# A scan and mixture-of-adapters kernel: new step priorities and latencies in its list scheduler, a row-tiled fp32 warm-up, and the constants' cast on GpSimd

## The chip, the cores and the metric

The kernel runs on one core of a Trainium2 chip. The metric is device time in microseconds (us) of one execution, and a kernel's time is the median of its runs. The profile is a trace of one execution. Its span is about 2 us shorter than the timed run of the same kernel (211.1 against 213.3 before), so times are compared with times and spans with spans.

Engines: PE is TensorE (PEld its weight loads), DVE is VectorE, ACT is ScalarE, POOL is GpSimd, SP is SyncE, which issues all large loads and stores.

## The reference

Cut to what matters:

```python
def _attn_ref(a, b):                    # a, b: [8, 6400, 128] fp32
    h = np.zeros((B, D))
    for t in range(S):
        h = a[:, t] * h + b[:, t]
        out[:, t] = h
def _moe_ref(x, w_gate, A, B):          # x: [51200, 128]; 8 experts of rank 16
    logits = x @ w_gate
    topk = ...                          # the 2 largest of 8
    w = softmax over the two
    for e in range(E):
        delta[mask] += w[mask, k, None] * ((x[mask] @ A[e]) @ B[e])
    return x + delta                    # x is the scan's output
```

## The kernel before

The 51,200 rows are cut into 100 tiles of 512. A tile `w` goes through these steps, each of four PE instructions or of one on another engine:

| step | engine | work |
|---|---|---|
| A, B | PE | fp32 transposes of `a` and `b` into PSUM |
| aev | ACT | copies the transposed `a` to SBUF |
| scan | DVE | the recurrence, gives `x` in fp16 |
| L | PE | logits, then small gating steps on DVE, POOL and ACT for up to four tiles together |
| Z | PE | `x` times all 8 `A` |
| mul | DVE, 13 of 100 on POOL | gates times Z |
| T, tev | PE, ACT | transposes the product, copies it |
| R, D | PE | `x` itself, then the product times `B`, both into the output's bank |
| oev | ACT (last ten: ACT or DVE) | copies the output tile; SP stores two tiles at a time |

The order of instructions on each engine isn't written by hand. A list scheduler simulates the kernel with a duration per step and a latency per engine, and takes the step that can start first, or among equals the one with the smallest key.

```python
        for op in ops.values():
            op.key = 300.0 * op.key - rank[op.name]
        # ... cut ...
        free = {e: 0.0 for e in self.sems}
        # ... cut: the pick ...
                    if best is None or (t + late, x[1].key) < best[:2]:
                        best = (t + late, x[1].key, e, x, t)
        # ... cut ...
            if op.dma:
                link = max(link, t + busy + 1500.0) + op.dma[2] / dma_rate
                end[op.name] = link + op.lat[e]
            else:
                end[op.name] = t + busy + op.lat[e]
```

```python
    KZ, KT, KR, KD = 8, 8.2, 8.6, 8.0
    PM = 6
    # ... cut ...
    stores = cut((), 2, (1, 1))          # stores of two tiles, the last two of one
    # ... cut ...
            lat = {"pe": 190.0, "dve": 120.0, "act": 150.0, "pool": 100.0, "sp": 100.0}
    # ... cut ...
        def heat(h):
            for _ in range(5):
                last = h.matmul(pB[1][:, :], warm_t[:, 0:128], warm_t[:, :])
            return last

        add("heat", "pe", -9, 2200.0, heat, ["wt"])
        add("idh", "dve", -8, 230.0, lambda h: h.tensor_copy(ident_h[:, :], ident_f[:, :]), ["id"])
        add("cst", "dve", -8, 300.0, lambda h: h.tensor_copy(cst_h[:, :], cst_f[:, :]), ["cst_in"])
    # ... cut ...
        def on_pool(w):
            return w % PM == 3 and 8 < w < NU - 16
    # ... cut: if on_pool(w), ACT copies pZ to SBUF (zev) and POOL multiplies ...
            add(f"Z{w}", "pe", w + KZ, 230.0, emit, [f"scan{w}", f"mul{w - NZ}", f"zev{w - NZ}", "cst"])
            add(f"R{w}", "pe", w + KR, 226.0, emit_x, [f"scan{w}", f"oev{w - NO}", "idh"])
            add(f"D{w}", "pe", w + KD, 226.0, emit_d, [f"R{w}", f"tev{w}", "cst"])
```

Of the kernel before, what the change touches and what calls it, by code (L numbers as in the profile page):

```python
# [7 lines left out]
F32 = mybir.dt.float32  # L8
# [22 lines left out]
class _Plan:  # L31
# [24 lines left out]
    def schedule(self, dma_rate):  # L56
# [16 lines left out]
        free = {e: 0.0 for e in self.sems}  # L73
# [7 lines left out]
        while todo:  # L81
# [20 lines left out]
            if op.dma:  # L102
                link = max(link, t + busy + 1500.0) + op.dma[2] / dma_rate
                end[op.name] = link + op.lat[e]
            else:
                end[op.name] = t + busy + op.lat[e]
# [36 lines left out]
def bass_associative_scan_2x2__then__mixture_of_adapters_kernel(  # L143
# [24 lines left out]
    KZ, KT, KR, KD = 8, 8.2, 8.6, 8.0  # L168
    PM = 6
# [31 lines left out]
    with ExitStack() as stack:  # L201
# [6 lines left out]
        warm_t = sb(nc.sbuf_tensor("warm_t", [128, UT], F16))  # L208
        warm = sb(nc.sbuf_tensor("warm", [128, 1], F32))
# [40 lines left out]
        def add(name, eng, key, busy, emit, deps=(), dma=None, bank=None):  # L250
            lat = {"pe": 190.0, "dve": 120.0, "act": 150.0, "pool": 100.0, "sp": 100.0}
            plan.add(name, eng, key, busy, lat, emit, deps, dma, bank)

        def add_dma(name, eng, key, emit, slot, nbytes, deps=()):
            if slot not in dma_sem:
                dma_sem[slot] = [sb(nc.semaphore("q_" + "_".join(map(str, slot)))), 0]
            dma_sem[slot][1] += 16
            sem, value = dma_sem[slot]
            add(name, eng, key, 650.0, lambda h: emit(h).then_inc(sem, 16), deps, (sem, value, nbytes))


        add("id0", "pool", -9, 200.0, lambda h: h.memset(ident_f[:, :], 0.0))
# [3 lines left out]
            -9,  # L266
# [21 lines left out]
        add("cst_in", "act", -9, 1800.0, lambda h: cst_load(h).then_inc(s_cst, 16), (), (s_cst, 48, 200000))  # L288
        add("w0", "dve", -9, 60.0, lambda h: h.memset(warm[:, :], 0.0))
        add("table", "act", -8, 1500.0, lambda h: h.activation(warm[:, :], warm[:, :], ACTF.Sigmoid), ["w0"])  # L290
        add("wt", "dve", -9, 60.0, lambda h: h.memset(warm_t[:, :], 0.0))

        def heat(h):
            for _ in range(5):
                last = h.matmul(pB[1][:, :], warm_t[:, 0:128], warm_t[:, :])
            return last

        add("heat", "pe", -9, 2200.0, heat, ["wt"])
        add("idh", "dve", -8, 230.0, lambda h: h.tensor_copy(ident_h[:, :], ident_f[:, :]), ["id"])
        add("cst", "dve", -8, 300.0, lambda h: h.tensor_copy(cst_h[:, :], cst_f[:, :]), ["cst_in"])  # L300
# [19 lines left out]
        def transposes(kind, w):  # L320
# [12 lines left out]
            add(f"{kind}{w}", "pe", w - (0.3 if kind == "A" else 0), 440.0, emit, [f"ld{kind.lower()}{load_of[w]}", free, "id"])  # L333

        def a_evac(w):
# [3 lines left out]
                w,  # L339
# [5 lines left out]
        def scan(w):  # L345
# [4 lines left out]
            def emit(h):  # L350
# [18 lines left out]
                f"scan{w}", "dve", w, 1140.0, emit, [f"aev{w}", f"B{w}", f"scan{w - 1}", f"R{w - XR}", f"Z{w - XR}", f"L{w - XR}"]  # L369
# [6 lines left out]
        def logits(w):  # L376
# [9 lines left out]
            add(f"L{w}", "pe", w + 1, 140.0, emit, [f"scan{w}", f"lev{k - 1}", "cst"], bank="TL")  # L386

        def gating(k):
# [3 lines left out]
            key = u0 + n + 0.5  # L392
# [8 lines left out]
            def bc(t):  # L401
# [5 lines left out]
                key,  # L407
# [81 lines left out]
                key,  # L489
# [5 lines left out]
        def z_mm(w):  # L495
# [5 lines left out]
            add(f"Z{w}", "pe", w + KZ, 230.0, emit, [f"scan{w}", f"mul{w - NZ}", f"zev{w - NZ}", "cst"])  # L501
# [4 lines left out]
        def z_mul(w):  # L506
# [5 lines left out]
            if on_pool(w):  # L512
# [4 lines left out]
                    w + 5.5,  # L517
# [5 lines left out]
            else:  # L523
# [6 lines left out]
                w + 5.5,  # L530
# [14 lines left out]
        def zw_tr(w):  # L545
            def emit(h):
# [7 lines left out]
                w + KT,  # L554
                225.0,
# [5 lines left out]
        def t_evac(w):  # L561
# [3 lines left out]
                w + 6,  # L565
# [6 lines left out]
        def delta(w):  # L572
# [24 lines left out]
            add(f"R{w}", "pe", w + KR, 226.0, emit_x, [f"scan{w}", f"oev{w - NO}", "idh"])  # L597
            add(f"D{w}", "pe", w + KD, 226.0, emit_d, [f"R{w}", f"tev{w}", "cst"])

        def o_evac(w):  # L600
            def emit(h):
# [6 lines left out]
                w + 6.5,  # L608
# [91 lines left out]
```

## Time and profile before

| | before |
|---|---|
| time, median (lowest to highest) | 213.32 us (212.79 to 214.33), 4 runs |
| span of the profile | 211.1 us |
| PE time without work, whole span | about 21 us |
| first transpose of `a` / first scan | 3.47 / 6.67 us |
| last group of `a` transposes / last D group / end | 194.0 / 207.3 / 211.1 us |
| last load landed | 184.9 us |

These lines are from the page of before: engine totals, the main DMA queue, the chain of work that ended last, and three groups of instructions (operation, shapes, count, then busy us and mean ns).

```profile
span 211.1 us, 7064 instructions
...
PE 202.7 (96%) x2805; PEld 192.9 (91%) x2805; DVE 187.7 (89%) x268; ACT 176.4 (84%) x371; POOL 99.1 (47%) x198
...
q1 hardware_dynamic: 40848, 78.65, 98.8%
...
PE 89%; DVE 3%; ACT 3%; DMA 2%; issue 1%; ACTq 0%; DVEq 0%
...
L358 DVE TENSOR_TENSOR_SCAN xT<-a_st,xT,pB 128x512 f16<-128x512 f32 x96 | 120.3, 1253 | 7.4 <-PE pB L327 3.2
...
L532 DVE TENSOR_TENSOR zw<-pZ,g 128x512 f16<-128x512 f32 x87 | 57.7, 675 | 2.8 <-ACT g L491 2.1
...
L532 POOL TENSOR_TENSOR zw<-z_sb,g 128x512 f16<-128x512 f32 x13 | 13.8, 1062 | 12.6 <-PE pTL L548 4.4
```

Three resources are nearly level: PE, DVE and the DMA queue. That "PE 96%" is not a distance to a limit: the records of matmuls overlap (that of an fp32 transpose lasts 277 ns on average, and back to back the next starts 109 ns after its start). The DMA queue counts as full at 389 to 400 GB/s in the windows below, and that measured rate is used here.

A stricter measure of PE is used throughout: **PE time lost** in a stretch is its length less the work issued in it. The work is the number of matmuls times the spacing that back-to-back ones show in the timeline: 109 ns for an fp32 transpose, 33 ns for a logits matmul, 56 ns for the others. This makes 1.90 us a tile and 190 us in all.

The windows of before follow. For each stretch they give its length, busy time and count for each engine, the granted clock, the DMA share and GB/s.

```profile
core 0: us, PE busy (x) PEld busy (x) DVE busy (x) ACT busy (x) POOL busy (x), PEclk, DMA share, GB/s
0.00:10.00 10.00, 7.05 (x50) 4.20 (x51) 3.86 (x10) 3.53 (x7) 0.70 (x6) 1.00 0.84 272
10.00:20.00 10.00, 9.32 (x104) 7.97 (x102) 9.73 (x19) 5.54 (x12) 3.56 (x12) 1.00 1.05 389
20.00:60.00 40.00, 39.70 (x504) 37.90 (x505) 38.99 (x49) 32.12 (x66) 17.06 (x34) 1.00 1.05 390
60.00:100.00 40.00, 40.00 (x576) 39.24 (x574) 37.39 (x52) 35.19 (x74) 21.27 (x40) 1.00 1.05 398
100.00:190.00 90.00, 89.95 (x1324) 88.32 (x1322) 83.52 (x112) 82.79 (x176) 51.03 (x94) 1.00 1.05 399
190.00:200.00 10.00, 9.72 (x162) 9.40 (x161) 9.87 (x23) 9.11 (x21) 4.45 (x13) 1.00 0.68 258
```

PE looks busy in all of these rows. By the stricter measure it lost 6.6 us by 10 us, 8.7 by 20, 11.7 by 60, 13.0 by 100 and 14.9 by 190. DMA runs full from 10 us until about 187 us and then has room.

The start in the timeline of before (start, length, engine, line, operation, and in brackets the idle time before it and what ended that):

```profile
3.47 0.98 PE L327 MATMUL pA<-ident_f,a_in 128*128 128x128 f32 x4
...
4.62 0.66 PE L327 MATMUL pB<-ident_f,b_in 128*128 128x128 f32 x4 [0.17 <-DMA b_in<-in_b_dram]
...
6.46 0.30 DVE L300 CAST cst_h<-cst_f 128x264 f16<-128x264 f32 x1 [4.72 <-DMA cst_f<-in_moe_B_dram]
...
6.67 1.21 DVE L358 TENSOR_TENSOR_SCAN xT<-a_st,pB 128x512 f16<-128x512 f32 x1
```

PE starts as soon as the first tile lands (3.4 us). DVE does the cast first, and its first scan comes behind it.

### The profile page before, as it was taken

Reading aid. Unit: us, or ns where it says so; the run is one execution under the profiler, and the core shown is the slowest. Engines: PE = TensorE matmul, PEld = TensorE weight load, DVE = VectorE, ACT = ScalarE, POOL = GpSimd, SP = SyncE. Lnnn points to the kernel's source line nnn. Section 1 sums busy time; section 2 is a strip of 40 time slices with the busy share of each in tenths; the row PEclk is TensorE's granted clock in tenths of the full one; section 3 lists DMA queues with packets and bytes.
Section 4 is the critical chain, followed back from the end, with each engine's and each line's share of the span. In section 5 each row is a group of like instructions: output and inputs, shape, how many; then the busy total and the mean of one; then the engine's idle time right before and its main releaser. Section 6 shows DMA issues by size and latency. Waiting matters only on the chain.

```text
span 211.1 us, 7064 instructions
## 1 busy us (share of the span) xinstructions
PE 202.7 (96%) x2805; PEld 192.9 (91%) x2805; DVE 187.7 (89%) x268; ACT 176.4 (84%) x371; POOL 99.1 (47%) x198
## 2 busy tenths in 40 slices
PE   7789999999999999999999999999999999999992
PEld 3579989999999999999999999999999999999881
DVE  1799999999999898998999899978999988999970
ACT  3256678888979879888999898999899999999994
POOL 1034261723545466265744386627554825644410
PEclk9999999999999999999999999999999999999997
DMA  6999999999999999999999999999999999998466
GB/s 180 378 389 383 389 383 387 390 395 388 397 394 397 398 398 402 397 393 398 397 399 398 403 401 398 398 400 398 400 399 402 402 397 398 398 396 339 166 257 227
DMA packets 42208, 79.23 MB, mean 375 GB/s; under 512 B 3648, under 2 KB 3776, under 8 KB 42176
## 3 DMA queue, kind: packets, MB, share of 16 engines
q1 hardware_dynamic: 40848, 78.65, 98.8%
q8 instruction: 22, 0.36, 0.7%
q10 hardware_dynamic: 1328, 0.14, 0.5%
q14 instruction: 10, 0.08, 0.1%
HBM read 52.56 MB, written 26.21 MB: 373 GB/s over the span
## 4 chain that ended last, share of the span: by engine, by line
PE 89%; DVE 3%; ACT 3%; DMA 2%; issue 1%; ACTq 0%; DVEq 0%
PE pA L327 21%; PE pB L327 21%; PE pO L587 11%; PE pO L575 10%; PE pZ L498 10%; PE pTL L548 10%; PE pTL L383 5%; DVE xT L358 3%; DMA cst_f<-in_moe_B_dram 2%; ACT outt L603 2%; ACT zwT L567 1%; PE pA L548 0%; ACT a_st L341 0%; ACTq L282 0%; ACTq L281 0%
## 5 line engine op out<-in xcount | busy, mean ns | idle before, releaser
L358 DVE TENSOR_TENSOR_SCAN xT<-a_st,xT,pB 128x512 f16<-128x512 f32 x96 | 120.3, 1253 | 7.4 <-PE pB L327 3.2
L341 ACT COPY a_st<-pA 128x512 f32<-128x512 f32 x100 | 60.1, 601 | 12.6 <-PE pA L327 8.1
L603 ACT COPY outt<-pO 128x512 f32<-128x512 f32 x100 | 59.1, 596 | 10.4 <-PE pO L587 8.6
L327 PE MATMUL pA<-ident_f,a_in 128*128 128x128 f32 x400 | 61.9, 277 | 0.9 <-DMA a_in<-in_a_dram 0.6
L327 PE MATMUL pB<-ident_f,b_in 128*128 128x128 f32 x400 | 61.6, 277 | 0.6 <-DMA b_in<-in_b_dram 0.4
L567 ACT COPY zwT<-pTL 128x512 f16<-128x512 f16 x95 | 56.6, 595 | 4.9 <-PE pTL L548 3.9
L532 DVE TENSOR_TENSOR zw<-pZ,g 128x512 f16<-128x512 f32 x87 | 57.7, 675 | 2.8 <-ACT g L491 2.1
L327 PEld LDWEIGHTS pA<-ident_f,a_in 128*128 128x128 f32 x400 | 42.7, 142 | 3.3 <-DMA a_in<-in_a_dram 1.7
L327 PEld LDWEIGHTS pB<-ident_f,b_in 128*128 128x128 f32 x400 | 42.7, 141 | 2.4 <-DMA b_in<-in_b_dram 0.9
L587 PE MATMUL pO<-cst_h,zwT 128*128 128x128 f16 x400 | 38.6, 218 | 0.8 <-ACT zwT L567 0.4
L575 PE MATMUL pO<-ident_h,xT 128*128 128x128 f16 x400 | 38.7, 220 | 0.3 <-ACT outt L603 0.2
L498 PE MATMUL pZ<-cst_h,xT 128*128 128x128 f16 x400 | 37.4, 219 | 0.0
L548 PE MATMUL pTL<-ident_h,zw 128*128 128x128 f16 x380 | 36.7, 219 | 0.0
L575 PEld LDWEIGHTS pO<-ident_h,xT 128*128 128x128 f16 x400 | 29.6, 114 | 1.1 <-ACT outt L603 0.6
L587 PEld LDWEIGHTS pO<-cst_h,zwT 128*128 128x128 f16 x400 | 27.6, 97 | 2.8 <-PE pO L575 0.7
L498 PEld LDWEIGHTS pZ<-cst_h,xT 128*128 128x128 f16 x400 | 28.6, 114 | 0.0
L548 PEld LDWEIGHTS pTL<-ident_h,zw 128*128 128x128 f16 x380 | 24.9, 98 | 0.7 <-issue 0.2
L383 PE MATMUL pTL<-cst_h,xT 128*128 128x8 f16 x400 | 23.3, 174 | 1.1 <-DVE xT L358 1.1
L383 PEld LDWEIGHTS pTL<-cst_h,xT 128*128 128x128 f16 x400 | 21.5, 117 | 2.3 <-DVE xT L358 1.8
L532 POOL TENSOR_TENSOR zw<-z_sb,g 128x512 f16<-128x512 f32 x13 | 13.8, 1062 | 12.6 <-PE pTL L548 4.4
L426 POOL TENSOR_TENSOR d_0<-Lg,m_0 128x128 f32<-128x128 f32 (+2 forms) x13 | 5.1, 394 | 18.6 <-DVE m_0 L418 18.5
L426 POOL TENSOR_TENSOR d_1<-Lg,m_1 128x128 f32<-128x128 f32 (+1 forms) x12 | 4.8, 403 | 18.8 <-DVE m_1 L418 18.8
(49 smaller groups left out, 136.7 us busy)
## 6 DMA issues: line engine op xcount, KB each, us to landing
a_in<-in_a_dram SPq DMA_DIRECT2D x49, 512.0 KB, 11.2
b_in<-in_b_dram SPq DMA_DIRECT2D x49, 512.0 KB, 11.3
out_dram<-outt SPq DMA_DIRECT2D x49, 512.0 KB, 11.2
a_in<-in_a_dram SPq DMA_DIRECT2D x2, 256.0 KB, 3.5
b_in<-in_b_dram SPq DMA_DIRECT2D x2, 256.0 KB, 4.0
out_dram<-outt SPq DMA_DIRECT2D x2, 256.0 KB, 2.1
cst_f<-in_moe_A_dram ACTq DMA_DIRECT2D x1, 64.0 KB, 4.3
cst_f<-in_moe_B_dram ACTq DMA_DIRECT2D x1, 64.0 KB, 4.8
```

The costliest lines, as they stand in the source:

```text
L327: last = h.transpose(view[:, i, :], ring[:, w % RING, i * 128 : (i + 1) * 128], ident_f[:, :])
L341: lambda h: h.copy(a_st[w % 2][:, :], pA[:, :]),
L358: last = h.tensor_tensor_scan(out=xT[:, x0 + lo : x0 + hi], data0=a_st[w % 2][:, lo:hi], data1=pB[w % 2][:, lo:hi], initial=init, op0=ALU. ...
L383: last = h.matmul(pL[:, c : c + E], x_block(w, i), wg_h)
L426: lambda h: h.tensor_tensor(out=v(d1[s]), in0=v(Lg[s]), in1=bc(m1[s]), op=ALU.subtract),
L498: last = h.matmul(pZ[w % NZ][:, i * 128 : (i + 1) * 128], x_block(w, i), Acat_h)
L532: lambda h: h.tensor_tensor(out=oview, in0=zview, in1=gview, op=ALU.mult),
L548: last = h.transpose(t_dst(w)[:, i * 128 : (i + 1) * 128], zw[w % 2][:, i, :], ident_h[:, :])
L567: lambda h: h.copy(zwT[w % 2][:, :], t_dst(w)),
L575: last = h.matmul(pO[w % NO][:, i * 128 : (i + 1) * 128], x_block(w, i), ident_h[:, :], start=i == 0, stop=False, skip_group_check=True,)
L587: last = h.matmul(pO[w % NO][:, i * 128 : (i + 1) * 128], zwT[w % 2][:, i * 128 : (i + 1) * 128], Bcat_h, start=False, stop=True, skip_gro ...
L603: return copy(outt[:, w % NOUT, :], pO[w % NO][:, :])
```

## The change: intent and diff

The intent has four parts.

- Give the scheduler measured latencies, and one tuned priority offset for each kind of step.
- Take the 13 multiplies and their extra copies off POOL and ACT.
- Warm PE with many small row-tiled fp32 transposes beside some matmuls.
- Cast the constants on the idle GpSimd, so that DVE's first scan need not stand behind the cast.

```diff
-        free = {e: 0.0 for e in self.sems}
+        free = {e: 700.0 for e in self.sems}
@@
-                end[op.name] = link + op.lat[e]
+                end[op.name] = link + op.lat[e] + sum(op.dma[3:])
@@
-    KZ, KT, KR, KD = 8, 8.2, 8.6, 8.0
-    PM = 6
+    KEY = {
+        "A": -1.1, "B": 0.0, "aev": 17.6, "scan": 0.1, "L": 1.0, "lev": -8.7, "gate": 2.0, "sig": -54.5, "Z": 6.3,
+        "mul": 8.5, "zev": 3.8, "T": 5.3, "tev": 2.4, "R": 10.8, "D": 5.4, "oev": 30.7,
+    }
+    PM = 1000
@@
-            lat = {"pe": 190.0, "dve": 120.0, "act": 150.0, "pool": 100.0, "sp": 100.0}
+            lat = {"pe": 205.0, "dve": 170.0, "act": 230.0, "pool": 130.0, "sp": 100.0}
@@  (a DMA issue: 650 -> 450 ns; constants' load: 200000 -> 140000 bytes and 3000 ns more)
@@  heat
-            for _ in range(5):
-                last = h.matmul(pB[1][:, :], warm_t[:, 0:128], warm_t[:, :])
+            for _ in range(2):
+                h.matmul(pB[1][:, :], warm_t[:, 0:128], warm_t[:, :])
+            for i in range(8):
+                for p, dst in ((0, pB[1]), (64, pO[0])):
+                    h.transpose(dst[:, i * 64 : (i + 1) * 64], warm_f[p : p + 64, 0:128],
+                                ident_f[p : p + 64, p : p + 64])
+            # ... cut: 4 matmuls of 128 columns ...
+            for i in range(4):
+                for p, dst in ((0, pB[1]), (32, pO[0]), (64, pB[0]), (96, pO[1])):
+                    h.transpose(dst[:, i * 32 : (i + 1) * 32], warm_f[p : p + 32, 0:128],
+                                ident_f[p : p + 32, p : p + 32])
+            # ... cut: 4 matmuls of 128 columns ...
-        add("heat", "pe", -9, 2200.0, heat, ["wt"])
-        add("cst", "dve", -8, 300.0, ...)
+        add("heat", "pe", -109, 2200.0, heat, ["wt", "wf", "id"])
+        add("cst", "pool", -108, 600.0, ...)
@@  (each step: w + its old constant -> w + KEY[kind]; durations 140/230/225/226 -> 132/224/224/224)
```

More of the change, by code (lines that the diff above doesn't have):

```diff
@@ L208, in bass_associative_scan_2x2__then__mixture_of_adapters_kernel @@
         warm_t = sb(nc.sbuf_tensor("warm_t", [128, UT], F16))
+        warm_f = sb(nc.sbuf_tensor("warm_f", [128, 128], F32))
         warm = sb(nc.sbuf_tensor("warm", [128, 1], F32))
@@ L258, in add_dma @@
             sem, value = dma_sem[slot]
-            add(name, eng, key, 650.0, lambda h: emit(h).then_inc(sem, 16), deps, (sem, value, nbytes))
-        add("id0", "pool", -9, 200.0, lambda h: h.memset(ident_f[:, :], 0.0))
+            add(name, eng, key, 450.0, lambda h: emit(h).then_inc(sem, 16), deps, (sem, value, nbytes))
+        add("id0", "pool", -109, 200.0, lambda h: h.memset(ident_f[:, :], 0.0))
         add(
@@ L265, in bass_associative_scan_2x2__then__mixture_of_adapters_kernel @@
             "pool",
-            -9,
+            -109,
             300.0,
@@ L286, in cst_load @@
             return h.dma_start(cst_f[:, E + 128 : E + 256], moe_B.rearrange("e r d -> (e r) d"))
-        add("cst_in", "act", -9, 1800.0, lambda h: cst_load(h).then_inc(s_cst, 16), (), (s_cst, 48, 200000))
-        add("w0", "dve", -9, 60.0, lambda h: h.memset(warm[:, :], 0.0))
-        add("table", "act", -8, 1500.0, lambda h: h.activation(warm[:, :], warm[:, :], ACTF.Sigmoid), ["w0"])
-        add("wt", "dve", -9, 60.0, lambda h: h.memset(warm_t[:, :], 0.0))
-        def heat(h):
-            for _ in range(5):
-                last = h.matmul(pB[1][:, :], warm_t[:, 0:128], warm_t[:, :])
-            return last
@@ L298, in bass_associative_scan_2x2__then__mixture_of_adapters_kernel @@
-        add("heat", "pe", -9, 2200.0, heat, ["wt"])
-        add("idh", "dve", -8, 230.0, lambda h: h.tensor_copy(ident_h[:, :], ident_f[:, :]), ["id"])
-        add("cst", "dve", -8, 300.0, lambda h: h.tensor_copy(cst_h[:, :], cst_f[:, :]), ["cst_in"])
+        add("cst_in", "act", -109, 1800.0, lambda h: cst_load(h).then_inc(s_cst, 16), (), (s_cst, 48, 140000, 3000.0))
+        add("w0", "dve", -109, 60.0, lambda h: h.memset(warm[:, :], 0.0))
+        add("table", "act", -108, 1500.0, lambda h: h.activation(warm[:, :], warm[:, :], ACTF.Sigmoid), ["w0"])
@@ new lines, in bass_associative_scan_2x2__then__mixture_of_adapters_kernel @@
+        add("wf", "pool", -109, 60.0, lambda h: h.memset(warm_f[:, :], 0.0))
+        add("wt", "dve", -109, 60.0, lambda h: h.memset(warm_t[:, :], 0.0))
+        def heat(h):
+            for _ in range(2):
+                h.matmul(pB[1][:, :], warm_t[:, 0:128], warm_t[:, :])
+            for i in range(8):
+                for p, dst in ((0, pB[1]), (64, pO[0])):
+                    h.transpose(
+                        dst[:, i * 64 : (i + 1) * 64],
+                        warm_f[p : p + 64, 0:128],
+                        ident_f[p : p + 64, p : p + 64],
+                    )
+            for i in range(4):
+                last = h.matmul(pB[1][:, i * 128 : (i + 1) * 128], warm_t[:, 0:128], warm_t[:, 0:128])
+            for i in range(4):
+                for p, dst in ((0, pB[1]), (32, pO[0]), (64, pB[0]), (96, pO[1])):
+                    h.transpose(
+                        dst[:, i * 32 : (i + 1) * 32],
+                        warm_f[p : p + 32, 0:128],
+                        ident_f[p : p + 32, p : p + 32],
+                    )
+            for i in range(4):
+                last = h.matmul(pB[1][:, i * 128 : (i + 1) * 128], warm_t[:, 0:128], warm_t[:, 0:128])
+            return last
@@ L303, in load @@
+        add("heat", "pe", -109, 2200.0, heat, ["wt", "wf", "id"])
+        add("idh", "dve", -108, 230.0, lambda h: h.tensor_copy(ident_h[:, :], ident_f[:, :]), ["id"])
+        add("cst", "pool", -108, 600.0, lambda h: h.tensor_copy(cst_h[:, :], cst_f[:, :]), ["cst_in"])
         def load(k):
@@ L332, in transposes @@
             free = f"aev{w - 1}" if kind == "A" else f"scan{w - 2}"
-            add(f"{kind}{w}", "pe", w - (0.3 if kind == "A" else 0), 440.0, emit, [f"ld{kind.lower()}{load_of[w]}", free, "id"])
+            add(f"{kind}{w}", "pe", w + KEY[kind], 440.0, emit, [f"ld{kind.lower()}{load_of[w]}", free, "id"])
         def a_evac(w):
@@ L338, in a_evac @@
                 "act",
-                w,
+                w + KEY["aev"],
                 480.0,
@@ L368, in scan @@
             add(
-                f"scan{w}", "dve", w, 1140.0, emit, [f"aev{w}", f"B{w}", f"scan{w - 1}", f"R{w - XR}", f"Z{w - XR}", f"L{w - XR}"]
+                f"scan{w}", "dve", w + KEY["scan"], 1140.0, emit, [f"aev{w}", f"B{w}", f"scan{w - 1}", f"R{w - XR}", f"Z{w - XR}", f"L{w - XR}"]
             )
@@ L384, in emit @@
                 return last
-            add(f"L{w}", "pe", w + 1, 140.0, emit, [f"scan{w}", f"lev{k - 1}", "cst"], bank="TL")
+            add(f"L{w}", "pe", w + KEY["L"], 132.0, emit, [f"scan{w}", f"lev{k - 1}", "cst"], bank="TL")
         def gating(k):
@@ L391, in gating @@
             s = k % 2
-            key = u0 + n + 0.5
+            key = u0 + n + KEY["gate"]
             ge = ("pool", "dve") if k < 2 or k >= len(groups) - GF else "pool"
@@ L406, in gating @@
                 "act",
-                key,
+                u0 + n + KEY["lev"],
                 170.0,
@@ L488, in gating @@
                 "act",
-                key,
+                u0 + n + KEY["sig"],
                 200.0,
@@ L499, in emit @@
                 return last
-            add(f"Z{w}", "pe", w + KZ, 230.0, emit, [f"scan{w}", f"mul{w - NZ}", f"zev{w - NZ}", "cst"])
+            add(f"Z{w}", "pe", w + KEY["Z"], 224.0, emit, [f"scan{w}", f"mul{w - NZ}", f"zev{w - NZ}", "cst"])
         def on_pool(w):
@@ L516, in z_mul @@
                     "act",
-                    w + 5.5,
+                    w + KEY["zev"],
                     480.0,
@@ L529, in z_mul @@
                 eng,
-                w + 5.5,
+                w + KEY["mul"],
                 busy,
@@ L553, in zw_tr @@
                 "pe",
-                w + KT,
-                225.0,
+                w + KEY["T"],
+                224.0,
                 emit,
@@ L564, in t_evac @@
                 "act",
-                w + 6,
+                w + KEY["tev"],
                 480.0,
@@ L595, in emit_d @@
                 return last
-            add(f"R{w}", "pe", w + KR, 226.0, emit_x, [f"scan{w}", f"oev{w - NO}", "idh"])
-            add(f"D{w}", "pe", w + KD, 226.0, emit_d, [f"R{w}", f"tev{w}", "cst"])
+            add(f"R{w}", "pe", w + KEY["R"], 224.0, emit_x, [f"scan{w}", f"oev{w - NO}", "idh"])
+            add(f"D{w}", "pe", w + KEY["D"], 224.0, emit_d, [f"R{w}", f"tev{w}", "cst"])
         def o_evac(w):
@@ L607, in o_evac @@
                 ("act", "dve") if w >= NU - TAIL else "act",
-                w + 6.5,
+                w + KEY["oev"],
                 {"act": 480.0, "dve": 600.0},
```

## The prediction

> **What bounds the kernel now.** Three resources are nearly level. The page's busy table has PE at 96%, DVE at 89% (187.7 us), ACT at 84% of a 211.1 us span; the DMA queue that carries loads and stores takes 98.8%.
> - PE: the timeline gives start-to-start times of 109 ns for a warm fp32 transpose, 56 ns for an fp16 matmul or transpose, 33 ns for a logits matmul. Summed: 1.90 us a tile, 190 us for 100 tiles. So PE is without work for about 21 us of the span. By ten-microsecond windows: 6.6 us in the first, 2.1 in the second, 3.0 in 20-60, 2.9 in 60-190, 0.7 in 190-200, the rest in the tail, of which 3.4 us is the last eviction and store.
> - DVE: a scan costs 1.19 us start to start, a gate multiply 0.58. The windows show DVE at 97% or more from 10 to 50 us and 83-98% from 70 us on: the kernel is DVE-bound early (it runs ahead with scans) and PE-bound afterwards.
> - DMA: 79.2 MB at the steady 400 GB/s is 198 us, plus a slow start: about 203 us at least. It is full until 187 us, then half empty: the last load lands at 184.9 us, while PE still has about 19.5 us of work.
>
> **What the change does.**
> 1. PM=1000 takes all 13 multiplies off POOL: 13 ACT copies go (601 ns each, 7.8 us of ACT), DVE gets 13 multiplies (+7.6 us). DVE work becomes about 191 us, level with PE's 190, so a stall of either will count.
> 2. The new order. PE's mix of steps is nearly unchanged; in the DVE order the multiplies come sooner (39 scans before multiply 24; 44 scans before). Counting both orders with the durations above, DVE and PE reach each eighth tile together, with about 10-11.5 us of PE time lost by the middle; before it was 13. I expect 1.5 to 3 us here.
> 3. Start: DVE now waits for the constants' cast (ready 6.46 us) before its first scan at 6.67. With the cast on POOL the scan need not wait. But the new warm-up waits for the identity (about 1.5 us) and holds 42 matmuls, so it may end near 5.5-6 us, after the first tile lands (3.4 and 4.6 us). Tile 2 lands only at 9.5 us; both kernels wait for it, so the start is worth 0 to 1 us. [...]the first four transposes take 0.98 us, later ones 0.66.
> 4. Tail: as many PE steps follow the last transpose of a as before, but they alternate better, and the last two output copies use ACT and DVE together: 0.5 to 1.5 us.
>
> Loads and stores move the same bytes.
>
> **Prediction.** 208.8 us (range 206.3 to 211.4). Faster by over 2%: 0.5; within 2%: 0.48; slower: 0.02.
>
> **What would show it.** DVE busy about 195 us, 94%; ACT about 168 us; no multiply on POOL; PE time lost by 100 us about 11 us in place of 13; last transpose of a at about 192 us in place of 194.0; first scan between 5.4 and 7.6 us; DMA windows after 190 us above 260 GB/s.
>
> **What would make it wrong.** DVE, now as loaded as PE, stalls on evictions and drags PE (210 or more). A warm-up that ends late or leaves PE cold delays everything. Or the old order's stalls were mostly avoidable and the new span approaches the 203 us of DMA (205).

The gains named come to 2 to 5.5 us.

## The result, and the profile after

| | before | after |
|---|---|---|
| time, median (lowest to highest) | 213.32 us (212.79 to 214.33) | 211.22 us (211.16 to 211.33) |
| ratio, 95% interval | | 0.990 (0.986 to 0.993) |
| span of the profile | 211.1 | 209.4 |
| first transpose of `a` / first scan | 3.47 / 6.67 | 5.13 / 7.15 |
| PE time lost by 10, 20, 60, 100, 190 us | 6.6, 8.7, 11.7, 13.0, 14.9 | 7.2, 9.0, 12.2, 12.8, 14.0 |
| last group of `a` transposes | 194.0 | 193.1 |
| last D group | 207.3 | 205.2 |

A ratio is the mean time of one kernel's fast runs over that of the other's fast runs of the same rounds, so it is not quite the ratio of the medians quoted. The kernel became 1.0% (2.1 us) faster, against a forecast of 4.4 us (208.8 us, against the 213.18 us that the kernel before had shown when the forecast was made). The outcome is "within 2%", to which the prediction gave 0.48.

The page of after, same lines:

```profile
span 209.4 us, 7147 instructions
...
PE 202.2 (97%) x2842; PEld 194.9 (93%) x2842; DVE 193.6 (92%) x279; ACT 170.2 (81%) x356; POOL 87.1 (42%) x190
...
q1 hardware_dynamic: 40848, 78.65, 99.8%
...
PE 87%; DVE 6%; ACT 2%; issue 2%; POOL 0%; DVEq 0%; POOLq 0%
...
L381 DVE TENSOR_TENSOR_SCAN xT<-a_st,xT,pB 128x512 f16<-128x512 f32 x96 | 120.2, 1252 | 2.7 <-PE pB L350 1.1
...
L555 DVE TENSOR_TENSOR zw<-pZ,g 128x512 f16<-128x512 f32 x100 | 66.9, 674 | 0.8 <-ACT a_st L364 0.2
```

No multiply is left on POOL, DVE rose by 5.9 us and ACT fell by 6.2, as intended. The windows of after, same columns:

```profile
0.00:10.00 10.00, 8.04 (x75) 6.10 (x76) 3.13 (x6) 3.17 (x6) 1.24 (x8) 1.00 0.88 273
10.00:20.00 10.00, 9.38 (x106) 8.53 (x107) 9.50 (x18) 5.49 (x13) 3.05 (x11) 1.00 1.05 387
20.00:60.00 40.00, 39.54 (x509) 37.45 (x508) 39.49 (x51) 31.36 (x64) 15.93 (x34) 1.00 1.05 389
60.00:100.00 40.00, 40.00 (x578) 39.51 (x576) 39.54 (x56) 35.39 (x75) 18.48 (x38) 1.00 1.05 398
100.00:190.00 90.00, 90.00 (x1339) 89.19 (x1338) 88.19 (x122) 79.05 (x169) 43.87 (x89) 1.00 1.05 399
190.00:200.00 10.00, 9.85 (x166) 9.47 (x164) 9.66 (x22) 9.79 (x23) 3.93 (x10) 1.00 0.72 270
```

PE issues 15 more matmuls between 100 and 190 us (1339 against 1324), and DVE is 98% busy there (93% before). The DMA column has not moved. The first row's larger PE count is the warm-up, not work. The timeline of after shows its cost:

```profile
5.13 1.06 PE L350 MATMUL pA<-ident_f,a_in 128*128 128x128 f32 x4
...
5.98 1.06 PE L350 MATMUL pB<-ident_f,b_in 128*128 128x128 f32 x4
...
6.20 0.40 POOL L323 CAST cst_h<-cst_f 128x264 f16<-128x264 f32 x1 [4.72 <-DMA cst_f<-in_moe_B_dram]
...
6.95 1.02 PE L350 MATMUL pA<-ident_f,a_in 128*128 128x128 f32 x4
7.15 1.22 DVE L381 TENSOR_TENSOR_SCAN xT<-a_st,pB 128x512 f16<-128x512 f32 x1 [5.42 <-PE pB L350]
```

The warm-up holds PE until 5.1 us, although the first tile landed at 3.6. PE is still cold (1.06 us for a group of four, against 0.66 at 4.62 us before). The cast no longer stands before the scan, but the scan now waits for the transposes and starts half a microsecond later than before.

### The profile page after: what moved, and what is told of

The parts are those of the page before. It is cut to its first block, busy times and chain, and to the rows that moved or that the text cites. A ratio compares the mean times of both kernels' runs of the same rounds, so it can differ in the third digit from the quotient of the medians.

```text
span 209.4 us, 7147 instructions
## 1 busy us (share of the span) xinstructions
PE 202.2 (97%) x2842; PEld 194.9 (93%) x2842; DVE 193.6 (92%) x279; ACT 170.2 (81%) x356; POOL 87.1 (42%) x190
## 4 chain that ended last, share of the span: by engine, by line
PE 87%; DVE 6%; ACT 2%; issue 2%; POOL 0%; DVEq 0%; POOLq 0%
PE pA L350 20%; PE pB L350 19%; PE pO L610 11%; PE pZ L521 10%; PE pO L598 10%; PE pTL L571 10%; DVE xT L381 6%; PE pTL L406 5%; ACT a_st L364 1%; ACT outt L626 1%; PE pB L300 0%; PE pB L303 0%; ACT zwT L590 0%; PE pA L571 0%; PE pB L312 0%
## 5 line engine op out<-in xcount | busy, mean ns | idle before, releaser
L555 DVE TENSOR_TENSOR zw<-pZ,g 128x512 f16<-128x512 f32 x100 | 66.9, 674 | 0.8 <-ACT a_st L364 0.2
L626 ACT COPY outt<-pO 128x512 f32<-128x512 f32 x98 | 57.8, 594 | 10.5 <-PE pO L610 9.1
L350 PEld LDWEIGHTS pB<-ident_f,b_in 128*128 128x128 f32 x400 | 44.1, 142 | 1.8 <-issue 1.1
L350 PEld LDWEIGHTS pA<-ident_f,a_in 128*128 128x128 f32 x400 | 43.3, 143 | 1.8 <-issue 1.3
L521 PE MATMUL pZ<-cst_h,xT 128*128 128x128 f16 x400 | 38.6, 219 | 0.0
L598 PEld LDWEIGHTS pO<-ident_h,xT 128*128 128x128 f16 x400 | 30.1, 114 | 0.6 <-ACT outt L626 0.3
L571 PEld LDWEIGHTS pTL<-ident_h,zw 128*128 128x128 f16 x380 | 25.7, 98 | 0.3
L406 PE MATMUL pTL<-cst_h,xT 128*128 128x8 f16 x400 | 22.0, 174 | 0.3 <-DVE xT L381 0.3
L406 PEld LDWEIGHTS pTL<-cst_h,xT 128*128 128x128 f16 x400 | 20.5, 117 | 0.8 <-DVE xT L381 0.8
L381 DVE TENSOR_TENSOR_SCAN xT<-a_st,pB 128x512 f16<-128x512 f32 (+1 forms) x8 | 7.5, 942 | 5.7 <-PE pB L350 5.4
```

The lines of the kernel that those rows point to most:

```text
L350: last = h.transpose(view[:, i, :], ring[:, w % RING, i * 128 : (i + 1) * 128], ident_f[:, :])
L381: last = h.tensor_tensor_scan(out=xT[:, x0 + lo : x0 + hi], data0=a_st[w % 2][:, lo:hi], data1=pB[w % 2][:, lo:hi], initial=init, op0=ALU. ...
L406: last = h.matmul(pL[:, c : c + E], x_block(w, i), wg_h)
L521: last = h.matmul(pZ[w % NZ][:, i * 128 : (i + 1) * 128], x_block(w, i), Acat_h)
L555: lambda h: h.tensor_tensor(out=oview, in0=zview, in1=gview, op=ALU.mult),
L571: last = h.transpose(t_dst(w)[:, i * 128 : (i + 1) * 128], zw[w % 2][:, i, :], ident_h[:, :])
```

## The experiments

Fourteen kernels ran, in four sets, on several chips. Each was timed against the kernel before in the same rounds; medians of different sets aren't from the same rounds. Each profile is one execution, and a kernel's own runs in one set spread by 0.2 to 2.7 us, so a small difference between two profiles is read here from where the events lie, and not from the total alone. "Landed" means that the last of the 16 semaphore increments of a load or store has come (the traces of before and after keep 2,496 for 156 transfers), and times from issue to landing count from the start of the issue.

| kernel | median us | before, same rounds | ratio (95% interval) | last D group | end of span |
|---|---|---|---|---|---|
| after | 211.22 | 213.32 | 0.990 (0.986 to 0.993) | 205.20 | 209.40 |
| a1_oldwarm | 210.34 | 213.22 | 0.987 (0.984 to 0.991) | 204.28 | 208.48 |
| a2_pm6 | 213.75 | 213.22 | 1.000 (0.996 to 1.004) | 206.72 | 212.08 |
| a3_castdve | 213.18 | 213.22 | 0.999 (0.996 to 1.002) | 204.68 | 211.05 |
| b1_pm | 213.82 | 213.22 | 1.002 (0.999 to 1.005) | 208.12 | 211.91 |
| c1_oldwarm_castdve | 210.36 | 213.13 | 0.988 (0.985 to 0.990) | 204.02 | 208.23 |
| c2_after_long | 212.50 | 213.13 | 0.997 (0.995 to 0.999) | 205.57 | 210.25 |
| d1_oldlat | 213.17 | 213.13 | 1.000 (0.998 to 1.002) | 207.31 | 211.46 |
| d2_oldkeys | 214.93 | 213.13 | 1.008 (1.006 to 1.010) | 208.76 | 212.96 |
| n1_lightpe | 209.25 | 212.93 | 0.983 (0.979 to 0.986) | 202.71 | 207.30 |
| n2_lightdve | 209.73 | 212.93 | 0.984 (0.981 to 0.987) | 202.94 | 208.04 |
| n3_lightboth | 209.13 | 212.93 | 0.982 (0.979 to 0.985) | 201.15 | 207.35 |
| f1_stores | 209.90 | 212.93 | 0.985 (0.982 to 0.988) | 204.32 | 208.36 |
| e1_fetch | 212.46 | 212.89 | 0.998 (0.993 to 1.002) | 205.14 | 210.47 |
| e2_nowarm | 210.81 | 212.89 | 0.990 (0.985 to 0.995) | 204.59 | 208.78 |

### a1_oldwarm: after, with the old warm-up

The order on all engines is that of after; only the warm-up differs.

```diff
-            for _ in range(2): ...            # and all row-tiled transposes
+            for _ in range(5):
+                last = h.matmul(pB[1][:, :], warm_t[:, 0:128], warm_t[:, :])
-        add("heat", "pe", -109, 2200.0, heat, ["wt", "wf", "id"])
+        add("heat", "pe", -109, 2200.0, heat, ["wt"])
```

> The changed kernel with the old warm-up alone (five fp16 matmuls that wait for nothing but their memset); the order of every other instruction on every engine is unchanged. Theory W (the new warm-up runs past the first landing and leaves PE cold): first transpose of a back from 5.13 us to about 3.5, PE warm by the first transposes of b (0.66 us for four instead of 1.06), PE time lost in the first ten microseconds about 6.4 us in place of 7.2, and the time falls by 0.6 to 1.2 us, to about 210.2. Rival (what I argued in the prediction): both kernels wait for the third tile's landing at 9.5 us anyway, so the start is made up by then, and the time stays within 0.3 us of the changed kernel's 211.2.

Measured: 210.34 us, 0.9 less than after. The first transpose starts at 3.65 us and the first scan at 5.32. PE has lost 6.2 us by 10 us (after: 7.2), 13.1 by 190 (14.0), and the last D group comes 0.92 us sooner (204.28). PE and DVE in the timeline of a1_oldwarm:

```profile
3.65 0.93 PE L332 MATMUL pA<-ident_f,a_in 128*128 128x128 f32 x4
4.54 0.66 PE L332 MATMUL pB<-ident_f,b_in 128*128 128x128 f32 x4
5.32 1.22 DVE L363 TENSOR_TENSOR_SCAN xT<-a_st,pB 128x512 f16<-128x512 f32 x1 [3.58 <-PE pB L332]
```

The lead gained at the start stays to the end: it is 1.0 us of PE time by 10 us, 0.9 by 20, 1.0 by 60 and 0.9 by 190. The rival fails at the landing it rests on. Tile 2 lands at 9.5 us (after) and 9.6 (a1_oldwarm), but by 9.5 us PE has started 32 of the tiles' matmuls and transposes in after and 44 in a1_oldwarm, and the third scan, tile 2's, starts at 11.21 against 10.30 us. The two kernels' intervals against before overlap, because before scatters, but their own runs don't (210.19 to 211.01, and 211.16 to 211.33). So the new warm-up costs about 0.9 us (the two were not timed in the same rounds, but the forecast was 0.6 to 1.2), and the rest of the change is worth 2.9 us by the medians.

### a2_pm6: after, with the 13 multiplies back on POOL

```diff
-    PM = 1000
+    PM = 6
```

> The changed kernel with 13 multiplies back on POOL (PM=6), new priorities. Theory P (the gain of the change after 60 us, where PE lost 1.2 us in 90-190 instead of 1.9, comes from freeing ACT of the 13 copies and taking away the slow 1.06 us POOL multiplies): slower than the changed kernel by 0.5 to 1.5 us, about 212.2. Rival D (the 13 multiplies made DVE the limit between 10 and 80 us, where it is 95 to 100% busy): faster by 0.5 to 1.5 us, about 210.2, with less PE time lost by 80 us than 12.6.

Measured: 213.75 us, no gain over before. The last D group is at 206.72, 1.5 us later than in after. About another 1.2 us went after PE had finished: the last three stores landed 3.3 to 3.8 us after issue, beside an instruction fetch at 208.5 us (more on this below). Two of its six runs took 212.3 and 212.4 us, so the profiled one (213.88) is of the slower kind. With these keys the multiplies are better on DVE.

### a3_castdve: after, with the cast on DVE

```diff
-        add("cst", "pool", -108, 600.0, ...)
+        add("cst", "dve", -108, 300.0, ...)
```

The scheduler puts the cast between the first and second scan, and some eight PE steps trade places.

> The changed kernel with the cast of the constants back on DVE, where the scheduler now puts it between the first and the second scan. Theory: the cast's engine is worth nothing once the first scan does not stand behind it: within 0.3 us of 211.2. Rival: the second scan is delayed by some 0.2 us or the logits and Z matmuls of the first tile come later, and 0.3 us or more are lost.

Measured: 213.18 us, 2.0 more than after, which taken alone would say that the GpSimd cast is worth 2 us. The profile says otherwise: PE lost less (13.5 us by 190, against 14.0) and its last D group came 0.5 us *sooner*. The time was lost after PE had ended. The DMA view of the last microseconds (203 to 212), first of after, then of a3_castdve, gives by queue the packets, MB and share, and by size the stores' KB and median us from issue to landing:

```profile
q1 hardware_dynamic: 906, 1.69, 50.4%
...
out_dram<-outt SPq DMA_DIRECT2D x2, 512.0 KB, 2.8
out_dram<-outt SPq DMA_DIRECT2D x2, 256.0 KB, 2.6
```

```profile
q1 hardware_dynamic: 832, 1.57, 46.9%
q8 instruction: 1, 0.02, 1.2%
...
out_dram<-outt SPq DMA_DIRECT2D x1, 512.0 KB, 5.0
out_dram<-outt SPq DMA_DIRECT2D x2, 256.0 KB, 4.8
```

In a3_castdve one packet of queue 8, which the page lists as "instruction", falls among the last stores. It is a fetch of 16 KB, at 205.4 us, and it took 1.76 us (the median of those in before and after is 1.07 and 1.06). The stores issued at 204.2, 205.0 and 205.7 landed at 209.3, 209.9 and 210.5, about 5 us later instead of 2.7. A store raises its semaphore 16 times, and the packed trace keeps the time of each. In a3_castdve the store issued at 204.2 us has 15 of them between 206.83 and 206.98 us, and the sixteenth at 209.27. In after all 16 of the store issued at 204.7 come between 207.34 and 207.53. So one increment in sixteen is late, and the rest are on time. Before and after have 22 such fetches, and this is the 23rd. There is one to about 260 PE instructions, weight loads counted (22 to 5,610 in before and to 5,684 in after; n3_lightboth below, with 600 fewer than a1_oldwarm, has 20; e1_fetch, with 96 more, has 23), so I take them for PE's instructions, and where they fall depends on how fast PE runs and on how many instructions stood before (in e1_fetch the first comes at 12.6 us, in a1_oldwarm at 18.2).

### b1_pm: before, with all multiplies on DVE

```diff
-    PM = 6
+    PM = 1000
```

> The kernel before with PM=1000 alone, old priorities, old latencies, old warm-up. If moving the multiplies is what gained (theory P): about 212.2, 1 us under before. If DVE is the limit (rival D): slower than before, 214 or more, with PE time lost by 80 us above 12.3. If only the new priorities make the move pay: between 213 and 214.

Measured: 213.82 us, no gain. PE had lost 12.1 us by 60 us (before 11.7) and 15.7 by 190 (14.9). With the old keys the move of the multiplies gains nothing.

### c1_oldwarm_castdve and c2_after_long: is it the cast, or the fetch?

c1 is a3_castdve with the old warm-up, thus with 74 fewer PE instructions. c2 is after with 32 more PE instructions in the warm-up and nothing else.

```diff
 # c1: a1_oldwarm, and
-        add("cst", "pool", -108, 600.0, ...)
+        add("cst", "dve", -108, 300.0, ...)
 # c2: after, 32-row warm-up transposes
-            for i in range(4):
+            for i in range(8):
```

> The kernel with the cast on DVE (213.18 us) but with the old warm-up, which has 74 PE instructions fewer; all other orders unchanged. In the run with the cast on DVE, PE finished 0.5 us sooner than in the changed kernel, and yet the span was 1.7 us longer: a 16 KB instruction fetch started at 205.4 us, took 1.76 us and the last three stores landed 4.5 to 5.1 us after their issue in place of 2.7. Theory F (that fetch among the last stores is the whole loss, and it is there because of where the program's length leaves the prefetch, not because of the cast): with fewer PE instructions no fetch after 200 us, last stores landing under 3 us after issue, and 210.0 to 210.6 us, as with the cast on POOL and the old warm-up (210.34). Rival C (the cast on DVE costs the 2 us by itself): 212.0 or more.

> The changed kernel with 16 more of the small row-tiled transposes in the warm-up (32 PE instructions more, some 0.3 us of start); nothing else changed. Theory F: the next instruction fetch now comes before the program ends, among the last stores, as with the cast on DVE: 212.5 to 213.7 us, last stores landing 4 us or more after issue. Rival C: only the longer warm-up counts, 211.3 to 211.7 us, no fetch after 200 us.

Measured: c1 took 210.36 us, the same as a1_oldwarm (210.34). It has 22 fetches, the last at 198.4 us, and its last stores landed 2.6 to 2.8 us after issue. So the engine of the cast is worth nothing that can be measured once the cast stands behind the first scan (here at 5.74 us), and the loss of a3_castdve is not the cast's. The cast in front of the first scan, as in the kernel before, was not run with the new order. c2 took 212.5 us, 1.3 more than after. Its first transpose came at 5.55 us (5.13), its last D group 0.4 us later, and a 23rd fetch at 203.7 us stood among the last stores, which then landed 3.1 to 3.4 us after issue. The forecast of 4 us or more was too high: of the 0.85 us that c2's span is longer, 0.4 is the later PE and 0.5 the later stores.

### d1_oldlat and d2_oldkeys: measured latencies alone, new priorities alone

Both are a1_oldwarm with one half of the scheduler's change undone.

```diff
 # d1: new KEY, old latencies, durations and DMA model
-        free = {e: 700.0 for e in self.sems}
+        free = {e: 0.0 for e in self.sems}
-            lat = {"pe": 205.0, "dve": 170.0, "act": 230.0, "pool": 130.0, "sp": 100.0}
+            lat = {"pe": 190.0, "dve": 120.0, "act": 150.0, "pool": 100.0, "sp": 100.0}
 # ... cut: DMA issue 650 ns, constants' load, durations 140/230/225/226 ...
 # d2: new latencies, old priorities
-        "A": -1.1, "B": 0.0, "aev": 17.6, "scan": 0.1, "L": 1.0, "lev": -8.7, "gate": 2.0, "sig": -54.5, "Z": 6.3,
-        "mul": 8.5, "zev": 3.8, "T": 5.3, "tev": 2.4, "R": 10.8, "D": 5.4, "oev": 30.7,
+        "A": -0.3, "B": 0.0, "aev": 0.0, "scan": 0.0, "L": 1.0, "lev": 0.5, "gate": 0.5, "sig": 0.5, "Z": 8.0,
+        "mul": 5.5, "zev": 5.5, "T": 8.2, "tev": 6.0, "R": 8.6, "D": 8.0, "oev": 6.5,
```

> Old warm-up, new priorities, multiplies on DVE, cast on POOL, but the scheduler's old latencies and durations. Theory K (the new priorities carry the gain of the order): 210.3 to 210.9, within 0.6 us of the kernel with the old warm-up (210.34). Rival L (the measured latencies carry it): 212 or more, PE time lost by 190 us near 15 in place of 13.1.

> Old warm-up, measured latencies, multiplies on DVE, cast on POOL, but the old priorities. Theory K: 212.5 to 213.8, near the kernel before with the multiplies on DVE (213.82), PE time lost by 190 us near 15. Rival L: 210.3 to 210.9. In both cases read the last PE step's start as well, since an instruction fetch may fall among the last stores.

Measured: 213.17 and 214.93 us, with 15.0 and 15.2 us of PE time lost by 190 us (a1_oldwarm 13.1). Neither half works alone. With the new keys the old latencies give no gain, and with the measured latencies the old keys are even worse than before. Keys, latencies and the move of the multiplies are one tuned set, and their parts can't be added up.

### n1_lightpe, n2_lightdve, n3_lightboth: what is left if PE or DVE has less to do?

n1 drops three of the four R matmuls of each tile, and n2 multiplies only half of the columns (the other half is zeroed once, by POOL). n3 does both. n1 and n3 are wrong; n2's result stayed within the tolerance. Loads and stores are the same.

```diff
 # n1: a1_oldwarm, emit_x
-                for i in range(Q):
+                for i in range(1):
 # n2: a1_oldwarm, z_mul
-            oview = zw[w % 2][:, :, :].rearrange("p q (e r) -> p q e r", e=E)
+            oview = zw[w % 2][:, 0 : Q // 2, :].rearrange("p q (e r) -> p q e r", e=E)
 # ... cut: gview and zview alike ...
```

> Wrong result on purpose: the old warm-up kernel (210.34 us) with three of the four matmuls that add x left out, same orders otherwise: 16.8 us less PE work (300 x 56 ns), nothing else changed. If PE alone sets the pace: down until the DMA floor, my estimate 203 to 205 us from 79.2 MB at 400 GB/s plus the slow start. If DVE is level with PE, as I argued: no more than 2 us down, 208 or more, with DVE at 95% or more in every window from 10 to 190 us.

> Wrong result on purpose: the old warm-up kernel with every multiply on DVE doing half of its columns, the other half left zero from the start: about 27 us less DVE work, same orders. If PE sets the pace: no more than 1 us down. If DVE shares the limit, above all from 20 to 60 us (PE time lost there 3.1 us): 1 to 2.5 us down, with PE time lost by 60 us under 10 in place of 11.2.

> Wrong result on purpose: both cuts together. If PE and DVE hold each other up, more is gained than the sum of the two: to the DMA floor of 203 to 205 us. If the loads and stores already set the pace: no more than either alone.

Measured: 209.25, 209.73 and 209.13 us, against 210.34 for a1_oldwarm. PE was relieved of 16.8 us (300 matmuls at 56 ns), DVE of 21 us of its busy time (193.6 to 172.3 in n2), and both together gained 1.2 us. n1 went as expected of a DVE level with PE: DVE is busy for 9.5 us or more of every ten from 10 to 190 us, and has 33% of the chain of waits (1% in a1_oldwarm). In n2 PE is back at 86% of that chain, with 10.6 us lost by 60 us, where under 10 was expected. n3 gained no more than n1, within the noise. Lines of the windows of n3_lightboth:

```profile
100.00:190.00 90.00, 84.38 (x1163) 79.15 (x1161) 75.34 (x120) 75.83 (x164) 42.87 (x87) 1.00 1.05 400
190.00:200.00 10.00, 9.37 (x142) 8.12 (x141) 7.71 (x25) 9.93 (x24) 2.89 (x8) 1.00 0.89 338
```

The share of the chain of waits, on n3_lightboth's page:

```profile
PE 49%; DMA 34%; ACT 8%; SPq 4%; issue 2%; DVE 1%; ACTq 0%
```

DMA, 2% of that chain before, not in it after and 6% in a1_oldwarm, is now 34%. It lies from 9 to 22 us and in most of the stretch from 98 to 168: there the lighter engines wait for a transfer rate that was there all along. From 168 us the chain runs over PE, from 185.9 to 193.5 over ACT, then over PE and ACT to the last copies. ACT had not been relieved, and was busy for 9.93 of the 10 us from 190 to 200 (above). So n3 bounds what faster PE and DVE could gain, but it isn't the floor of DMA; a run with ACT relieved too was not made. SyncE's last load issue and its last stretch of store issues, in the timelines of before, after and n3_lightboth, stand at the same place in all three:

```profile
173.55 1.17 SPq L311 DMA_DIRECT2D b_in<-in_b_dram  x1
174.76 33.94 SPq L621 DMA_DIRECT2D out_dram<-outt  x17
```

```profile
173.66 1.24 SPq L334 DMA_DIRECT2D b_in<-in_b_dram  x1
174.95 31.64 SPq L644 DMA_DIRECT2D out_dram<-outt  x17
```

```profile
173.40 1.28 SPq L318 DMA_DIRECT2D b_in<-in_b_dram  x1
174.73 28.01 SPq L628 DMA_DIRECT2D out_dram<-outt  x17
```

The last load landed at 184.9 us in before, 185.3 in after, 185.4 in a1_oldwarm and 185.0 in n3_lightboth, however fast the engines are: some 70 MB go through between 10 and 187 us in each, at 396 GB/s. No engine can be ahead of its loads. After the last landing, a chain of transposes, scan, multiply, D and stores is still to be done. In n3_lightboth PE did end 3.1 us sooner than in a1_oldwarm (201.15 against 204.28), but its last stores took 4.5 to 4.7 us to land instead of 2.6 to 2.8, so that the span ended only 1.1 us sooner. Again it is mostly one of the 16 increments: of the last store 15 had come by 205.28 us, the sixteenth at 206.81. In a1_oldwarm that lag shrank from 1.8 us to 0.02 between the stores issued at 196.2 and 203.8, where DMA had moved 295 GB/s from 190 to 200 us; in n3_lightboth it moved 338.

The 16 increments also show what bytes over rate leaves out: by the end of the loads they are far apart. Of the last load of before the first came at 179.45 us and the last at 184.88; in n3_lightboth at 179.48 and 184.97. In e1_fetch (below) PE began on a load only after its last increment: 15 had come by 13.52 us, the last at 14.85, and PE started at 14.89. Why the sixteen drift apart isn't shown.

### f1_stores: six single-tile stores at the end

```diff
-    stores = cut((), 2, (1, 1))
+    stores = cut((), 2, (1, 1, 1, 1, 1, 1))
```

> The old warm-up kernel with the last six tiles stored one by one instead of two pairs and two single ones; right result, orders of PE, DVE, ACT and POOL unchanged. In the old warm-up kernel the last MB is issued from 203.8 us on and lands 2.6 to 2.8 us after each issue, close to the full rate, and the last store lands 3.4 us after the last PE step begins. Theory: the DMA starts on the earlier tile of each pair 0.7 us sooner, and 0.3 to 0.7 us are gained, about 209.8. Rival: the time from issue to landing is latency, not queueing, or more issues on the queue take up the gain: within 0.2 us of 210.34.

Measured: 209.90 us, the lowest of the correct kernels with all the work. Its interval (0.982 to 0.988) overlaps that of a1_oldwarm (0.984 to 0.991) and the spans are 208.36 and 208.48, so the two are not separated. Its PE was cold for longer than a1_oldwarm's (groups of four at 1.11, 1.11, 1.12 and 0.85 us, until about 7.3 us), with the same warm-up.

### e1_fetch: the instruction fetch moved, the warm-up's work not

The same columns of warm-up, in 53 small matmuls instead of 5 large ones: 96 more PE instructions.

```diff
-            for _ in range(5):
-                last = h.matmul(pB[1][:, :], warm_t[:, 0:128], warm_t[:, :])
+            for _ in range(53):
+                last = h.matmul(pB[1][:, 0:48], warm_t[:, 0:128], warm_t[:, 0:48])
```

> The kernel with the old warm-up (210.34 us, last instruction fetch at 198.7 us), but the warm-up's five 512-column matmuls cut into 53 of 48 columns: 2544 columns in place of 2560, so about the same PE time, and 96 PE instructions more; nothing else changed. Theory F (a fetch among the last stores is the whole loss in the cast-on-DVE run): a fetch between 202 and 207 us, last stores landing 3.3 us or more after issue in place of 2.7, first transpose of a and last PE step within 0.5 us of the old warm-up kernel's (3.65 and 204.5), and 211.3 to 212.7 us. Rival: the fetch does not matter, or none comes: 210.0 to 210.8.

Measured: 212.46 us, 2.1 more than a1_oldwarm, with the first transpose at 3.38 us. Two things show. A 23rd fetch stands at 205.7 us among the last stores, as in a3_castdve. The same DMA view of the last microseconds:

```profile
q8 instruction: 1, 0.02, 0.7%
...
out_dram<-outt SPq DMA_DIRECT2D x2, 512.0 KB, 3.7
out_dram<-outt SPq DMA_DIRECT2D x2, 256.0 KB, 3.8
```

The stretch from the last D group to the end grew by 1.1 us (5.3 against 4.2). The second thing I had not expected: the last D group itself came 0.86 us later, where I had allowed 0.5 at most. The first fetch moved from 18.2 us to 12.6, and the next pair of loads landed 1.2 us later (`a` at 14.85 instead of 13.63, `b` at 16.20 instead of 14.98). Of this `a`, 15 of the 16 increments had come by 13.52 us. PE has no tiles in hand then, and waits. PE in the timeline of e1_fetch:

```profile
14.89 0.66 PE L332 MATMUL pA<-ident_f,a_in 128*128 128x128 f32 x4 [1.03 <-DMA a_in<-in_a_dram]
...
16.24 0.66 PE L332 MATMUL pB<-ident_f,b_in 128*128 128x128 f32 x4 [0.58 <-DMA b_in<-in_b_dram]
```

In after the first fetch is at 16.0 us (a1_oldwarm 18.2), and `b` of tiles 8 and 9 lands at 18.83 instead of 17.70. But here PE had tiles in hand: it lost 1.8 us from 10 to 20 us and 3.2 from 20 to 60, and in a1_oldwarm 1.9 and 3.2, so this earlier fetch cost nothing that shows.

### e2_nowarm: no warm-up to speak of

```diff
-            for _ in range(5):
-                last = h.matmul(pB[1][:, :], warm_t[:, 0:128], warm_t[:, :])
+            for _ in range(1):
+                last = h.matmul(pB[1][:, 0:48], warm_t[:, 0:128], warm_t[:, 0:48])
```

> The old warm-up kernel with the warm-up cut to one 48-column matmul; 8 PE instructions fewer, nothing else changed. It tells a late start from a cold PE. With the new warm-up PE began its first transposes 1.5 us late and ran the first twelve at half rate until 7.8 us. If the cold PE is what cost 0.9 us: the first transposes start near 3.5 us but take 1 us a group of four till about 7 us, PE time lost by 10 us is 7 or more, and the time is 211 or more. If the late start cost it: within 0.3 us of 210.34.

Measured: 210.81 us. Neither forecast held. PE starts on time (3.58 us) and is cold until about 8.7 us (groups of four transposes at 1.12, 1.11, 1.12 and 1.07 us). It lost 6.6 us by 10 us, between a1_oldwarm's 6.2 and after's 7.2, and the last D group (204.59) also lies between. So a cold but punctual PE seems to cost less than the new warm-up. As an estimate from these losses, about 0.3 of the new warm-up's 1.0 us is the cold PE and 0.7 the late start. The times alone don't settle it: the intervals of a1_oldwarm, e2_nowarm and after against before overlap one another.

## Why the prediction was right or wrong

The direction was right and the size was wrong: -2.1 us measured, -4.4 forecast. The step that failed is the third, the start, which had a wait wrong; in the second, the order, the size was too high, and the floor of DMA was too low. The profiles let the sum be checked term by term. Their spans differ by 1.7 us:

| term | predicted, us saved | measured, us saved | how measured |
|---|---|---|---|
| start, to 10 us | 0 to 1 | -0.6 | PE lost 6.6 before, 7.2 after |
| order, 10 to 190 us | 1.5 to 3 | 1.5 | PE lost 8.3 before, 6.8 after |
| tail, last `a` transposes to last D group | 0.5 to 1.5, as one term | 1.2 | 13.31 us before, 12.14 after |
| from the last D group to the end | in the term above | -0.4 | 3.77 us before, 4.20 after |
| not in any term | 0.65 | 0 | 4.4 less the terms' midpoints |

**The start failed.** "The start is worth 0 to 1 us" assumed that a late end of the warm-up is hidden, because both kernels wait for tile 2. It isn't hidden. The warm-up's end at 5.1 us delays the first scan (7.15 us, against 5.32 in a1_oldwarm), and PE, still cold until 7.8 us, hasn't caught up when tile 2 lands at 9.5: tile 2's scan starts at 11.21 us against 10.30. The lost time stays lost until the end: old warm-up alone, 0.9 us better. The prediction did name this risk ("a warm-up that ends late or leaves PE cold delays everything") but gave it no number in the sum. Against the midpoint of the start's range this is the largest single miss, 1.1 us of the 2.7 by which the spans' change (1.7) falls short of the forecast.

**The order was in its range, at the lower edge, and came elsewhere than predicted.** I expected 2 us less lost by 100 us (11 instead of 13). It was 12.8 (0.7 us of it the worse start), and from 20 to 60 us PE even lost slightly more than before (3.2 against 3.0). The gain came between 60 and 190 us and in the tail. Counting instructions in each order gave the mix of the work and not the waits between engines. With the 13 multiplies DVE is busy for 79.0 of the 80 us from 20 to 100 (76.4 before). That explains only part: with half of the multiplies' work gone (n2) PE still lost 3.0 us there, against 3.8 in after, and the rest stays open. The experiments agree: no part of the scheduler's change gains alone.

**The tail was right in size, in part by luck:** 1.2 us, less 0.4 given back by the stores (the last two landed 2.6 us after issue, against 2.0 and 2.2 before), within 0.5 to 1.5. But the last two output copies do not use ACT and DVE together. Both are on ACT; DVE took two earlier ones, at 201.52 and 203.97 us. That the better alternation gave the 1.2 us was not tested.

**The last 0.65 us had no term behind it.** The text's own midpoints sum to 3.75, and the forecast of 208.8 was set below that.

**The floor of DMA was set too low.** "About 203 us at least" as a span is right as bytes over rate, but no run came near it. With 16.8 us of PE work and 21 us of DVE work taken away, the span is 207.35 us and the time 209.13, still above the 208.8 forecast. As an estimate from n3_lightboth's own numbers: 203, plus 1.6 for the ten microseconds at 338 instead of 400 GB/s, plus 2.0 by which its last stores land late, makes 206.6 of the 207.35. The outputs of the last tiles do not come early enough to keep the queue full to its end. Before's span is only 3.7 us above that of n3_lightboth, so that a forecast of 4.4 us asked for more than this removal of work gave.

**Right:** DVE at 193.6 us, 92% (about 195, 94% predicted); ACT 170.2 (168); no multiply on POOL; first scan at 7.15 (5.4 to 7.6); last transposes of `a` at 193.1 (192); DMA after 190 us at 270 GB/s and more (above 260); the slow PE at the start. Groups of four fp32 transposes that are cold throughout take 1.06 to 1.12 us and warm ones 0.66 (213 against 109 ns from one transpose to the next), and the same old warm-up had PE warm by 4.5 us in one profile (a1_oldwarm) and by 7.3 in another (f1_stores). What sets the moment was not shown. The cast's engine is worth nothing once the cast stands behind the first scan (c1_oldwarm_castdve); what moving it from in front of the scan is worth was not run alone.

**What stays open.** Which of the 16 DMA engines carries an instruction fetch isn't in the trace. That one of them falls behind is my reading of two things, and was not shown directly. Beside a fetch one of a store's 16 increments comes 0.5 (c2_after_long) to 2.3 us (a3_castdve) after the other 15. And in the last microsecond of a3_castdve at most about 27 GB/s still move, about a sixteenth of 400. The stores are late whenever a fetch falls among the last of them (a2_pm6, a3_castdve, c2_after_long, e1_fetch) and land in 2.6 to 2.8 us where none does (after, c1_oldwarm_castdve). In n3_lightboth one increment lags by 1.5 us with no fetch among the last three stores; where that lag began wasn't traced. Why the kernel before scatters between 212.4 and 215.1 us, when after stays within 0.2, was not found.

The version to keep is the change without its new warm-up: 210.34 us (a1_oldwarm) or 209.90 (f1_stores), both with every run below all runs of before and after, though after was timed in other rounds.

## What to carry to other kernels

Before counting on saved engine time, find where the kernel ends if the engines had less to do: a kernel with part of the work removed bounds the gain in one run, and bytes over rate gave a span some 4 us below what this one reached. A warm-up should end before the first tile lands (here a late one cost 0.9 us), and its instruction count matters too, since it shifts the instruction fetches against the loads and stores (e1_fetch: the first from 18.2 to 12.6 us, the last from 198.7 to 205.7, and 2.1 us lost). When a small edit costs 2 us, compare when PE ends and when the stores land before blaming the edit: here a cast looked 2 us dear, and it was a fetch among the last stores.
